# Cosformer attention and token/channel mixer: tokens laid five to a row on 64 partitions and four on the other 64

## The chip, the cores and the metric

The kernel runs on one core of one Trainium2 chip. The metric is the device time of one execution in microseconds (us); lower is better. A profile of one execution stands beside the times. Its span is the time from the first to the last instruction; the execution's own time is a little longer. Engines are named as in the profile: PE (TensorE matmul), PEld (its weight load), DVE (VectorE), ACT (ScalarE), POOL (GpSimd), SP (SyncE, which here issues most DMAs); "POOLq" and "SPq" are their queues of DMA issues.

## The reference, cut to what matters

Eight batches, eight heads, 576 tokens, head dimension 64. Queries and keys become features of width 128, a linear attention follows, and its output goes through a mixer over tokens and one over channels.

```python
cos_w, sin_w = cos(pi/2 * pos / 576), sin(pi/2 * pos / 576)       # per token
phi(x) = concat([relu(x) * cos_w, relu(x) * sin_w])               # 64 -> 128
kv  = einsum('bhsf,bhsd->bhfd', phi(k), v)
z   = sum over s of phi(k)
x   = einsum('bhsf,bhfd->bhsd', phi(q), kv) / (phi(q) . z + 1e-6) # -> [8, 576, 512]
u   = x + (relu(x^T @ w_tok1) @ w_tok2)^T                         # 576 -> 256 -> 576, tokens
out = u + relu(u @ w_ch1) @ w_ch2                                 # 512 -> 1536 -> 512, channels
```

q, k, v and the output are float32 in HBM; the matmuls take bf16.

## The kernel before

**Tokens.** 576 tokens are 4 x 128 + 64. The first 512 (`SM`) lie four to a row (`R = 4`): partition p holds tokens 4p to 4p+3, and "chunk" ci (0 to 3) is the token ci of every row. The last 64 (`ST`) are chunk `R`, the tail. `load_main` (L85) brings a batch's 512 tokens of a tensor in one DMA over 128 rows, with runs of 1024 B for each head and row. `load_tail` (L91) brings its 64 tail tokens in another DMA with runs of 256 B: an even batch into rows 0 to 63 of a tail tile, an odd batch into rows 64 to 127 of the same tile. So a pair of batches shares a tail tile, and from batch 2 on one feature instruction over 128 rows serves the tails of both.

**Front of a batch** (`class Front`). `feature` (L247) computes one half (cos or sin) of the features of one chunk of q or k: on DVE, or on ACT with `on_act`. `values` (L267) casts v into `v_aug`, which has a column of ones; `kv` (L310) accumulates phi(k)^T v on PE; `kv_out` copies it to SBUF. Queries are turned to have features on the partitions: on PE for batches 0 and 1 (`q_trans`, L335), by a DMA transpose on SP for the others (`q_trans_dma`, L351). `num` (L356) multiplies them with kv and divides; `tok1` and `tok2` are the token mixer, `u_trans_dma` and `tail_trans_dma` (L437, L442) turn its result u for the channel mixer.

**Channel mixer** (`class Channel`). A batch has 12 c steps (`c_main`, u^T by w_ch1, 1536 wide in blocks of 128, ReLU on ACT) and then o steps (`o_step`, two matmuls of 512 columns by w_ch2 each). When a chunk is complete, DVE adds u and SP issues the store. The tails of a pair go through the channel mixer together, with the odd batch.

**Order.** The kernel runs under a manual schedule: each engine takes its instructions in the order in which the program emits them. `Front.pieces` (L461) is a list of (slot, piece): the pieces of batch b+1 are emitted behind step `slot` of batch b's channel mixer (slots 0 to 11 are c steps, `C`; from `O = NCH = 12` they are o steps). The tokens' chunks go in `ORDER = (0, 1, 2, R, 3)`. Loads for later batches are emitted in the main loop (L725 to L748) behind given steps; all go to SP's queue. Batch 0's front is `first_front` (L621), the lead-in; four weight loads for w_ch1 are issued on POOL behind k of batch 0 (L188, L192), and three for w_ch2 (L194) behind q of batch 1. `permute_tok2` (L210) casts w_tok2 and orders its columns by chunk, on ACT.

**Batch 1.** Its pieces are in the plan of L471 to L481. `KS`, `QS` are features of k and q, `QT` the turning on PE, `V` values, `KV` the product, `before.tok2` the token mixer's second half of batch 0.

Of the kernel before, what the change touches and what calls it, by code (L numbers as in the profile page):

```python
# [16 lines left out]
def kernel(  # L17
# [67 lines left out]
    def load_main(dst, src, b, lo=0, hi=H, eng=nc.sync):  # L85
        return eng.dma_start(
            out=dst[:, lo:hi, 0:R * D].rearrange("p h (r d) -> p h r d", r=R),
            in_=src[b, lo:hi, 0:SM, :].rearrange("h (p r) d -> p h r d", r=R))


    def load_tail(dst, src, b):  # L91
        return nc.sync.dma_start(out=dst[half(b % 2)],
                                 in_=src[b, :, SM:S, :].rearrange("h s d -> s h d"))

    def tiles():
        return tuple(io.tile([P, H, R * D], F32, name=n) for n in ("qt", "vt", "kt"))

    def tail_tiles():
        return tuple(io.tile([P, H, D], F32, name=n) for n in ("qtt", "vtt", "ktt"))

    io_tiles, io_tails = {0: tiles()}, {0: tail_tiles()}
    qt0, vt0, kt0 = io_tiles[0]
    qtt0, vtt0, ktt0 = io_tails[0]
    load_main(qt0, q, 0, 0, HH)
    load_main(qt0, q, 0, HH, H, nc.scalar)
    load_tail(qtt0, q, 0)
    load_main(kt0, k, 0, 0, HH)
    k_done = load_main(kt0, k, 0, HH, H)
    load_tail(ktt0, k, 0)
    load_main(vt0, v, 0, 0, HH)  # L110
    load_tail(vtt0, v, 0)
    load_main(vt0, v, 0, HH, H)

# [4 lines left out]
    nc.sync.dma_start(out=w_tok1n, in_=moe_w_tok1[0:SM, :].rearrange("(p r) t -> p r t", r=R))  # L118
# [14 lines left out]
    nc.gpsimd.iota(pos_i[:, 0:R], pattern=[[1, R]], base=0, channel_multiplier=R)  # L133
    for g in range(2):
        nc.gpsimd.iota(pos_i[half(g), R:NSC], pattern=[[1, 1]], base=SM, channel_multiplier=1)
# [19 lines left out]
    v_augs, x_tails = [], []  # L155
    for i in range(2):
        va = const.tile([P, NSC, H, DP], BF16, name=f"v_aug{i}")
        nc.vector.memset(va[:, 0:R, :, D:D1], 1.0)
        nc.vector.memset(va[half(1 - i), R, :, :], 0.0)
        nc.vector.memset(va[half(i), R, :, D:D1], 1.0)  # L160
        v_augs.append(va)
        xt = const.tile([P, Dm], BF16, name=f"x_tail{i}")
        nc.vector.memset(xt[half(1 - i), :], 0.0)
        x_tails.append(xt)

    class Tail:

        def __init__(self, pair):
            self.qt, self.vt, self.kt = io_tails[pair]
            self.kp = twos.tile([P, H, 2, D], BF16, name="kp_tail")  # L170
            self.qp = once.tile([P, H, 2, D], BF16, name="qp_tail")
            self.qpT = twos.tile([P, H, P], BF16, name="qpT_tail")
# [7 lines left out]
    for t in (tail0.kp, tail0.qp):  # L180
        nc.gpsimd.memset(t[half(1)], 0.0)
    for g in range(2):
        nc.gpsimd.dma_start(out=w_tail1[half(g), :], in_=moe_w_tok1[SM:S, :])
# [9 lines left out]
    def load_w_ch2(behind):  # L193
        done = [nc.gpsimd.dma_start(  # L194
            out=w_ch2[:, ki:ki + 4, :],
            in_=moe_w_ch2[ki * P:(ki + 4) * P, :].rearrange("(n t) d -> t n d", t=P))
            for ki in range(0, NCH, 4)]
        after(done[0], behind)
        return done
# [10 lines left out]
    def permute_tok2(ki):  # L210
        nc.scalar.copy(w_tok2[:, ki, 0:SM].rearrange("t (r p) -> t r p", r=R),
                       w_tok2n[:, ki, 0:SM].rearrange("t (p r) -> t r p", r=R))
        nc.scalar.copy(w_tok2[:, ki, SM:].rearrange("t (g s) -> t g s", g=2),
                       w_tok2n[:, ki, None, SM:S].to_broadcast([P, 2, ST]))


    class Front:
        def __init__(self, b, res, tail):
# [4 lines left out]


            self.alone = b < 2
            self.kp, self.qp = {}, {}
# [4 lines left out]

        def k_of(self, ci):
            return self.kp[ci] if ci < R else self.tail.kp

        def q_of(self, ci):
            return self.qp[ci] if ci < R else self.tail.qp
# [10 lines left out]
        def feature(self, which, ci, j, heads=(0, H), on_act=False):  # L247
            lo, hi = heads
            w = (cos_t, sin_t)[j][:, ci:ci + 1]
            if ci < R:  # L250
                dst, src = (self.kp, self.kt) if which == "k" else (self.qp, self.qt)
                if ci not in dst:
                    dst[ci] = phi.tile([P, H, 2, D], BF16, name=which + "p")
                o_ap = dst[ci][:, lo:hi, j, :]
                i_ap = src[:, lo:hi, ci * D:(ci + 1) * D]
            else:
                t = self.tail
                dst, src = (t.kp, t.kt) if which == "k" else (t.qp, t.qt)
                rows = self.rows if self.alone else slice(0, P)
                w, o_ap, i_ap = w[rows], dst[rows, lo:hi, j, :], src[rows, lo:hi, :]  # L260
            if on_act:
                nc.scalar.activation(o_ap, i_ap, AF.Relu, bias=bias0[0:w.shape[0]], scale=w)
            else:
                nc.vector.tensor_scalar(o_ap, i_ap, scalar1=w, scalar2=0.0,  # L264
                                        op0=ALU.mult, op1=ALU.max)

        def values(self, ci, eng, heads=(0, H)):  # L267
            lo, hi = heads
            if ci < R:
                src = self.vt[:, lo:hi, ci * D:(ci + 1) * D]  # L270
            else:
                src = self.tail.vt[self.rows, lo:hi, :]
            dst = self.va[self.rows_of(ci), ci, lo:hi, 0:D]
            if eng is nc.scalar:
                nc.scalar.copy(dst, src)  # L275
            else:
                eng.tensor_copy(dst, src)

        def ksum(self, ci, heads=(0, H)):
# [5 lines left out]
            for h in range(*heads):  # L285
                nc.tensor.matmul(self.ks_ps[:, h:h + 1],
                                 self.k_of(ci)[:, h, :, :].rearrange("p a b -> p (a b)"),
# [22 lines left out]
        def kv(self, ci, halves=(0, 1)):  # L310
# [8 lines left out]
            for g in halves:  # L319
                for j in range(HH):  # L320
                    nc.tensor.matmul(self.kv_ps[g][:, j * DP:j * DP + D1],  # L321
                                     self.k_of(ci)[:, g * HH + j, :, :]
# [13 lines left out]
        def q_trans(self, ci, heads=(0, H), eng=nc.scalar):  # L336
            lo, hi = heads
            if hi - lo == H:
                qT_ps = ps_at.tile([P, H, P], BF16, name="qT_ps", tag="at")
            else:  # L340
                qT_ps = ps_mm.tile([P, HH, P], BF16, name="qT_ps", tag="mm")
            for h in range(lo, hi):
                nc.tensor.transpose(qT_ps[:, h - lo, :],
                                    self.q_of(ci)[:, h, :, :].rearrange("p a b -> p (a b)"), ident)
            dst = self.qpT[:, ci * H + lo:ci * H + hi, :] if ci < R else self.tail.qpT[:, lo:hi, :]
# [5 lines left out]
        def q_trans_dma(self, ci):  # L351
            dst = self.qpT[:, ci * H:(ci + 1) * H, :] if ci < R else self.tail.qpT
            nc.sync.dma_start_transpose(out=dst,
                                        in_=self.q_of(ci).rearrange("p h a b -> p (h a b)"))
# [90 lines left out]
        def k_side(self, ci, on_act=False):  # L445
            self.feature("k", ci, 0)
            self.feature("k", ci, 1, on_act=on_act)

        def q_side(self, ci, on_act=False):
            self.feature("q", ci, 0)  # L450
            self.feature("q", ci, 1, on_act=on_act)
# [9 lines left out]
        def pieces(self, b, before):  # L461
# [6 lines left out]
            if first:  # L468

                last = NCH - 1  # L470
                plan = [(4, KS, 0), (5, KS, 1, True), (6, KS, 2, True), (6, KS, 3, True), (7, KS, R),  # L471
                        (8, QS, 0), (9, QS, 1), (9, QT, 0), (10, QS, 2), (10, QT, 1)]
                plan += [(last, *what) for what in (
                    (QS, 3, True), (QT, 2, (0, H), nc.vector), (before.tok2, 2, None, False),
                    (QS, R, True), (QT, 3), (before.tok2, 3, None, False),
                    (QT, R, (0, H), nc.vector), (before.tok2, R, None, False))]
                plan += [(last, V, ci, eng) for ci, eng in enumerate(
                    (nc.gpsimd, nc.gpsimd, nc.scalar, nc.scalar, nc.vector))]
                plan += [(last, KV, ci) for ci in range(NSC)]
                plan.append((last, self.kv_out))  # L480
                plan += [(5, before.tok2, 0, ps_at, False), (7, before.tok2, 1, ps_at, False)]  # L481
            else:
                plan = [(C + at, V, ci, nc.scalar) for ci, at in enumerate((-1, -1, 0, 1, 2))]
                plan += [(C + at, KS, ci) for ci, at in enumerate((0, 0, 1, 2, 2))
                         if ci < R or not odd]
                for ci, at in zip(ORDER, (1, 2, 3, 4, 5)):
                    if ci < R or not odd:
                        plan += [(C + at, QS, ci), (C + at, self.q_trans_dma, ci)]
# [6 lines left out]
            elif odd:  # L495
                at, mix, t = (C + 8, C + 9, C + 11, O + 1, O + 3), O + 4, O + 8
# [20 lines left out]
    class Channel:  # L517
# [39 lines left out]
        def o_step(self, ci, lo, hi, cols=slice(0, Dm)):  # L557
# [12 lines left out]
            if ci < R:  # L570
                nc.sync.dma_start(
                    out=out[b, 0:SM, cols].rearrange("(p r) d -> p r d", r=R)[:, ci, :], in_=o_sb)
                return
            for g in range(2):
                nc.sync.dma_start(out=out[b - 1 + g, SM:S, cols], in_=o_sb[half(g)])
# [206 lines left out]
```

## Time and profile before

Three executions took 276.12, 276.8 and 278.76 us; the median is 276.8.

| | |
|---|---|
| profiled execution | 275.45 us, span 273.6, 5130 instructions |
| granted PE clock | 1.00 throughout |
| HBM read, written | 35.85 MB, 9.44 MB |
| mean DMA rate | 196 GB/s |
| DMA packets | 91816, of them 59409 under 512 B |

Where the time lies by stage: the lead-in runs to about 24 us, where batch 0's c steps begin; its o steps begin at 43.95; from there a batch takes some 30 us (a pair 60.3); the last matmul ends at 270.0.

The page's table of engines gives busy time, its share of the span and the count of instructions. The costliest groups of PE show what it works on:

```profile
L564 PE MATMUL o_ps<-w_ch,h1T 128*128 128x512 bf16 (+1 forms) x396 | 94.8, 372 | 0.0
L531 PE MATMUL c_ps<-uT,w_ch 128*128 128x512 bf16 (+2 forms) x384 | 91.6, 372 | 1.0 <-DMA uT<-u_bf 1.0
```

Such a line has the kernel's line number, the engine and operation, the tiles written and read, shapes and count; then the busy time in us and the mean ns of one; then the engine's idle time ahead of the group and what ended most of it.

The chain of waits follows the work back from the last instruction, at each step to what released it. An answer over windows has, for each stretch of the span, the busy time and number of instructions of each engine, PE's granted clock, the mean share in which the 16 DMA engines were busy (it can be above 1, since packets overlap), and the bytes moved.

### The profile page before, as it was taken

What the parts mean: (1) busy time and instruction counts of PE and PEld (TensorE: products, weight loads), DVE (VectorE), ACT (ScalarE), POOL (GpSimd) and SP (SyncE); (2) the same over time, 40 slices, a digit from 0 to 9 for tenths busy, and PEclk for the clock granted to TensorE, in tenths of its full rate; (3) what the DMA queues carried; (4) which work ended last, traced back from release to release, by engine and by line L of the source; (5) the groups of instructions that cost most, each with busy time, mean ns of one, the idle gap of its engine ahead of it and who ended that gap; (6) DMA issues with size and microseconds to landing.
All of it is one profiled execution on the core that took longest, in us unless ns stands there. A gap on an engine that the chain in (4) does not pass through costs nothing.

```text
span 273.6 us, 5130 instructions
## 1 busy us (share of the span) xinstructions
PE 261.6 (96%) x2050; PEld 138.7 (51%) x2050; DVE 164.7 (60%) x375; ACT 129.8 (47%) x229; POOL 11.2 (4%) x24
## 2 busy tenths in 40 slices
PE   7989987999899999999999999999999999999994
PEld 2665354446554454445654455446644455435543
DVE  6973775774876396659566487659466577720022
ACT  4955982067525184156626183347606372426500
POOL 6400230000000000000000000000000000000000
PEclk9999999999999999999999999999999999999999
DMA  7999999738995897968993969669994361180032
GB/s 222 344 266 283 317 179 283 245 88 264 284 253 185 247 221 191 323 140 233 208 311 79 270 193 259 220 151 237 211 304 119 115 117 38 42 210 0 2 98 94
DMA packets 91816, 53.68 MB, mean 196 GB/s; under 512 B 59409, under 2 KB 86929, under 8 KB 91793
## 3 DMA queue, kind: packets, MB, share of 16 engines
q1 hardware_dynamic: 88432, 49.62, 65.4%
q0 software_dynamic: 2832, 3.21, 7.1%
q10 hardware_dynamic: 528, 0.52, 0.6%
q8 instruction: 16, 0.26, 0.4%
q14 instruction: 8, 0.06, 0.1%
HBM read 35.85 MB, written 9.44 MB: 166 GB/s over the span
## 4 chain that ended last, share of the span: by engine, by line
PE 80%; DMA 7%; DVE 7%; ACT 2%; issue 1%; SPq 0%; DVEq 0%
PE o_ps L564 31%; PE c_ps L531 23%; PE b_ps L385 6%; PE u_ps L409 5%; PE num_ps L362 4%; PE ct_ps L551 4%; DMA qpT<-qp 4%; PE kv_ps L321 3%; DVE qp L264 2%; DMA uT<-u_bf 2%; DMA qt<-in_q_dram 2%; DVE kp L264 2%; PE idle_ps L205 1%; PE c_ps L541 1%; DVE u_sb L412 1%
## 5 line engine op out<-in xcount | busy, mean ns | idle before, releaser
L564 PE MATMUL o_ps<-w_ch,h1T 128*128 128x512 bf16 (+1 forms) x396 | 94.8, 372 | 0.0
L531 PE MATMUL c_ps<-uT,w_ch 128*128 128x512 bf16 (+2 forms) x384 | 91.6, 372 | 1.0 <-DMA uT<-u_bf 1.0
L535 ACT ACTIVATE h1T<-c_ps 128x512 bf16<-128x512 f32 x93 | 55.4, 598 | 57.1 <-PE c_ps L531 56.9
L564 PEld LDWEIGHTS <-h1T 128*128 128x128 bf16 x396 | 37.0, 97 | 38.8
L531 PEld LDWEIGHTS <-w_ch 128*128 128x128 bf16 x384 | 33.3, 97 | 31.2 <-DMA uT<-u_bf 2.0
L569 DVE TENSOR_TENSOR o_sb<-o_ps,u_sb 128x512 f32<-128x512 f32 (+1 forms) x33 | 22.2, 673 | 32.7 <-PE o_ps L564 32.7
L412 DVE TENSOR_TENSOR u_sb<-u_ps,x_sb 128x512 f32<-128x512 f32 x32 | 22.0, 689 | 7.3 <-PE u_ps L409 6.8
L416 ACT CAST u_bf<-u_sb 128x512 bf16<-128x512 f32 x28 | 17.3, 618 | 17.8 <-DVE u_sb L412 16.1
L390 ACT ACTIVATE B<-b_ps 128x512 bf16<-128x512 f32 x8 | 4.8, 597 | 39.5 <-PE b_ps L385 39.5
L409 PE MATMUL u_ps<-B,w_tok 128*128 128x512 bf16 x80 | 22.5, 379 | 0.0
L372 DVE TENSOR_TENSOR x_sb<-num_ps,den 128x512 bf16<-128x512 f32 x28 | 19.4, 691 | 1.0
L551 PEld LDWEIGHTS <-w_ch 128*128 128x128 bf16 x192 | 14.0, 98 | 9.2
L264 DVE TENSOR_SCALAR qp<-qt,cos_t 128x512 bf16<-128x512 f32 (+1 forms) x35 | 15.9, 453 | 4.6 <-DMA qt<-in_q_dram 4.6
L385 PE MATMUL b_ps<-x_sb,w_tok 128*128 128x512 bf16 x64 | 17.9, 379 | 0.0
L264 DVE TENSOR_SCALAR kp<-kt,cos_t 128x512 bf16<-128x512 f32 x32 | 15.2, 480 | 3.9 <-DMA kt<-in_k_dram 3.9
L551 PE MATMUL ct_ps<-uT_tail,w_ch 128*128 128x128 bf16 x192 | 17.2, 219 | 0.0
L275 ACT CAST v_aug<-vt 128x512 bf16<-128x512 f32 (+1 forms) x30 | 16.7, 586 | 0.1
L264 DVE TENSOR_SCALAR qp<-qt,sin_t 128x512 bf16<-128x512 f32 (+1 forms) x34 | 15.7, 460 | 0.0
L362 PEld LDWEIGHTS <-qpT 128*128 128x128 bf16 x256 | 11.5, 98 | 7.1 <-DMA qpT<-qp 1.5
L362 PE MATMUL num_ps<-kv_sb,qpT 128*128 128x65 bf16 x256 | 13.1, 193 | 1.7 <-DMA qpT<-qp 0.7
L569 DVE TENSOR_TENSOR o_sb<-o_ps,u_tail 128x512 f32<-128x512 f32 x4 | 2.8, 692 | 20.0 <-PE o_ps L564 20.0
L321 PE MATMUL kv_ps<-v_aug,kp 128*128 128x65 bf16 x256 | 12.5, 193 | 2.2 <-ACT v_aug L275 1.7
(96 smaller groups left out, 220.9 us busy)
## 6 DMA issues: line engine op xcount, KB each, us to landing
out_dram<-o_sb SPq DMA_DIRECT2D x31, 256.0 KB, 2.9
kt<-in_k_dram SPq DMA_DIRECT2D x7, 1024.0 KB, 6.9
qt<-in_q_dram SPq DMA_DIRECT2D x7, 1024.0 KB, 8.6
vt<-in_v_dram SPq DMA_DIRECT2D x7, 1024.0 KB, 6.5
w_ch<-in_moe_w_ch_dram POOLq DMA_DIRECT2D x4, 384.0 KB, 10.4
w_ch<-in_moe_w_ch_dram POOLq DMA_DIRECT2D x3, 512.0 KB, 8.3
out_dram<-o_sb SPq DMA_DIRECT2D x10, 128.0 KB, 2.3
qtt<-in_q_dram SPq DMA_DIRECT2D x8, 128.0 KB, 5.9
```

The source lines that it names most:

```text
L264: nc.vector.tensor_scalar(o_ap, i_ap, scalar1=w, scalar2=0.0, op0=ALU.mult, op1=ALU.max)
L321: nc.tensor.matmul(self.kv_ps[g][:, j * DP:j * DP + D1], self.k_of(ci)[:, g * HH + j, :, :] .rearrange("p a b -> p (a b)"), self.va[:, ci, ...
L362: nc.tensor.matmul(num_ps[:, g, j * DP:j * DP + D1], self.qT_of(ci, h), self.kv_sb[g][:, j, 0:D1], start=True, stop=True)
L372: nc.vector.tensor_mul(self.x_of(ci)[rows].rearrange("p (g j d) -> p g j d", g=2, j=HH), nv[:, :, :, 0:D], den.to_broadcast([rows.stop - r ...
L385: nc.tensor.matmul(self.b1_ps[mi], w, self.x_of(ci), start=(ci == ORDER[0]), stop=(ci == ORDER[-1]))
L409: nc.tensor.matmul(u_ps, w_tok2[:, ki, ci * P:(ci + 1) * P], self.B1[:, ki, :], start=(ki == 0), stop=(ki == NT - 1))
L412: nc.vector.tensor_add(u, u_ps[rows], self.x_of(ci)[rows])
L531: nc.tensor.matmul(c_ps[:, lo:hi], w_ch1[:, ki, mi * P:(mi + 1) * P], uT[:, lo // P:hi // P, ki, :], start=(ki == 0), stop=(ki == NCC - 1))
L535: nc.scalar.activation(self.h1T[:, mi, :], c_ps, AF.Relu)
L551: nc.tensor.matmul(self.ct_ps[:, mi % R, :], w_ch1[:, ki, mi * P:(mi + 1) * P], self.tail.uT[:, ki, :], start=(mi % R == 0 and ki == 0), s ...
L564: nc.tensor.matmul(o_ps, h, w_ch2[:, ki, cols], start=ki == 0, stop=ki == NCH - 1)
L569: nc.vector.tensor_add(o_sb, o_ps, u)
```

## The change

- **Layout.** Rows 0 to 63 hold five tokens each (tokens 0 to 319), rows 64 to 127 four each (320 to 575). Chunk 4 (`R`) is now the fifth token of rows 0 to 63, in every batch. Each load of q, k or v is two DMAs of 64 rows, with runs of 1280 B and 1024 B; there are no tail tiles and no tail loads. w_tok1's load and every 128-row store are two DMAs of 64 rows as well. The tables of positions, the tail of w_tok1 and the order of w_tok2's columns follow (`permute_tok2` has three ACT instructions per block instead of two).
- **Tail work.** Each batch computes the features of its own chunk R on 64 rows, and each odd batch too has its own transpose of them. The tiles `kp_tail` and `qpT_tail` become two constant tiles each, whose unused parts are zeroed once on DVE in the setup (four memsets, among them two of 128 rows); the two memsets on POOL at L181 go.
- **Batch 1's pieces.** The sin features of k's chunks 0 to 3 and of q's chunks 2 and 3 go to POOL, that of q's chunk 1 to ACT; values 0 to 3 all go to POOL. The k features come one or two slots earlier. The three issues of w_ch2's load on POOL are emitted in slot 6, behind the k features. The pieces of `before.tok2` move, and its chunk R comes behind `kv_out`.
- **Odd batches.** The third, fourth and fifth num pieces, the token mixer and the turning of u come one slot earlier.
- **Third batch's query.** Its load (batch 2) is emitted one o step later, at `NCH + 17`, behind one more store.

```diff
-    def load_main(dst, src, b, lo=0, hi=H, eng=nc.sync):
-        return eng.dma_start(
-            out=dst[:, lo:hi, 0:R * D].rearrange("p h (r d) -> p h r d", r=R),
-            in_=src[b, lo:hi, 0:SM, :].rearrange("h (p r) d -> p h r d", r=R))
-    def load_tail(dst, src, b):
-        return nc.sync.dma_start(out=dst[half(b % 2)],
-                                 in_=src[b, :, SM:S, :].rearrange("h s d -> s h d"))
+    SL = ST * NSC
+    HALVES = ((half(0), slice(0, SL), NSC), (half(1), slice(SL, S), R))
+    def load(dst, src, b, lo=0, hi=H, eng=nc.sync):
+        return [eng.dma_start(out=dst[rows, lo:hi, 0:r * D],
+                              in_=src[b, lo:hi, toks, :].rearrange("h (p r) d -> p h (r d)", r=r))
+                for rows, toks, r in HALVES]
+    def by_rows(ap, rows, toks, r):
+        return ap[toks, :].rearrange("(p r) d -> p r d", r=r)
...
-    nc.sync.dma_start(out=w_tok1n, in_=moe_w_tok1[0:SM, :].rearrange("(p r) t -> p r t", r=R))
+    for half_of in HALVES:
+        nc.sync.dma_start(out=w_tok1n[half_of[0]], in_=by_rows(moe_w_tok1, *half_of)[:, 0:R, :])
...
+        kp = const.tile([P, H, 2, D], BF16, name=f"kp_tail{i}")
+        nc.vector.memset(kp[half(1)], 0.0)
+        kp_tails.append(kp)
+        qpT = const.tile([P, H, P], BF16, name=f"qpT_tail{i}")
+        nc.vector.memset(qpT, 0.0)
+        qpT_tails.append(qpT)
...
-    for t in (tail0.kp, tail0.qp):
-        nc.gpsimd.memset(t[half(1)], 0.0)
...
-        nc.scalar.copy(w_tok2[:, ki, 0:SM].rearrange("t (r p) -> t r p", r=R),
-                       w_tok2n[:, ki, 0:SM].rearrange("t (p r) -> t r p", r=R))
-        nc.scalar.copy(w_tok2[:, ki, SM:].rearrange("t (g s) -> t g s", g=2),
-                       w_tok2n[:, ki, None, SM:S].to_broadcast([P, 2, ST]))
+        main = w_tok2[:, ki, 0:SM].rearrange("t (r p) -> t r p", r=R)
+        for rows, toks, r in HALVES:
+            nat = w_tok2n[:, ki, toks].rearrange("t (p r) -> t r p", r=r)
+            nc.scalar.copy(main[:, :, rows], nat[:, 0:R, :])
+            if r > R:
+                nc.scalar.copy(w_tok2[:, ki, SM:].rearrange("t (g s) -> t g s", g=2),
+                               nat[:, R:r, :].to_broadcast([P, 2, ST]))
...
-                plan = [(4, KS, 0), (5, KS, 1, True), (6, KS, 2, True), (6, KS, 3, True), (7, KS, R),
-                        (8, QS, 0), (9, QS, 1), (9, QT, 0), (10, QS, 2), (10, QT, 1)]
-                plan += [(last, *what) for what in (
-                    (QS, 3, True), (QT, 2, (0, H), nc.vector), (before.tok2, 2, None, False),
-                    (QS, R, True), (QT, 3), (before.tok2, 3, None, False),
-                    (QT, R, (0, H), nc.vector), (before.tok2, R, None, False))]
-                plan += [(last, V, ci, eng) for ci, eng in enumerate(
-                    (nc.gpsimd, nc.gpsimd, nc.scalar, nc.scalar, nc.vector))]
-                plan += [(last, KV, ci) for ci in range(NSC)]
-                plan.append((last, self.kv_out))
-                plan += [(5, before.tok2, 0, ps_at, False), (7, before.tok2, 1, ps_at, False)]
+                dve, act, pool = nc.vector, nc.scalar, nc.gpsimd
+                T0, every = before.tok2, (0, H)
+                plan = [(3, KS, 0, pool), (4, KS, 1, pool), (5, T0, 0, ps_at, False),
+                        (5, KS, 2, pool), (6, KS, 3, pool), (6, KS, R), (6, load_w_ch2),
+                        (7, T0, 1, ps_at, False), (8, QS, 0), (8, QS, 1, act),
+                        (9, QT, 0), (9, QS, 2, pool), (10, QT, 1, every, dve), (10, QS, 3, pool),
+                        (11, QT, 2), (11, QS, R), (11, T0, 2, None, False),
+                        (11, QT, 3, every, dve), (11, T0, 3, None, False), (11, QT, R, every, dve)]
+                plan += [(11, V, ci, pool) for ci in range(R)]
+                plan.append((11, V, R, dve))
+                plan += [(11, KV, ci) for ci in range(NSC)]
+                plan += [(11, self.kv_out), (11, T0, R, None, False)]
...
-                at, mix, t = (C + 8, C + 9, C + 11, O + 1, O + 3), O + 4, O + 8
+                at, mix, t = (C + 8, C + 9, C + 10, C + 11, O + 2), O + 3, O + 7
...
-            if ci < R:
-                nc.sync.dma_start(
-                    out=out[b, 0:SM, cols].rearrange("(p r) d -> p r d", r=R)[:, ci, :], in_=o_sb)
-                return
-            for g in range(2):
-                nc.sync.dma_start(out=out[b - 1 + g, SM:S, cols], in_=o_sb[half(g)])
+            for g, half_of in enumerate(HALVES):
+                of = (out[b], *half_of) if ci < R else (out[b - 1 + g], *HALVES[0])
+                nc.sync.dma_start(out=by_rows(*of)[:, ci, cols], in_=o_sb[half(g)])
...
-            if b == 0 and i == NCH + 16:
+            if b == 0 and i == NCH + 17:
                 load_batch(2, "q")
```

## The prediction

> **What bounds the kernel now.** I read the page's busy shares and chain first, then the span in stretches, then single rows where TensorE (PE) idles. The page:
>
> ```profile
> PE 261.6 (96%) x2050; PEld 138.7 (51%) x2050; DVE 164.7 (60%) x375; ACT 129.8 (47%) x229; POOL 11.2 (4%) x24
> PE 80%; DMA 7%; DVE 7%; ACT 2%; issue 1%; SPq 0%; DVEq 0%
> ```
>
> PE is the bound: 12 of 273.6 us are idle, and 3.6 of those are the last add and stores. The stretches (window, length, busy time of PE, PEld, DVE, ACT, POOL with counts, granted clock, DMA share, GB/s) say where the rest is:
>
> ```profile
> 5.00:20.00 15.00, 13.35 (x226) 9.09 (x224) 12.33 (x36) 11.57 (x23) 3.21 (x4) 1.00 1.13 312
> 30.00:43.90 13.90, 10.79 (x111) 6.17 (x110) 10.16 (x20) 11.43 (x18) 3.88 (x5) 1.00 1.11 220
> 60.00:74.00 14.00, 12.44 (x134) 7.89 (x134) 9.04 (x22) 8.31 (x16) 0.00 (x0) 1.00 0.97 264
> 95.00:155.40 60.40, 60.27 (x453) 31.28 (x452) 39.73 (x89) 28.64 (x51) 0.00 (x0) 1.00 0.82 216
> ```
>
> 1.65 us in the lead-in, 3.11 in the stage of batch 1's pieces, 1.56 where batch 2 waits for q, almost nothing over a pair of batches. In the first two the DMA share is above 1.1: there, bytes and their rate are the limit. The rows that end the waits (start, us, engine, what, idle before and its end):
>
> ```profile
> 18.92 1.13 ACT L211 CAST w_tok<-u_sb 128x512 bf16<-128x512 f32 x1 [2.07 <-DMA u_sb<-in_moe_w_tok_dram]
> 28.58 0.49 DVE L264 TENSOR_SCALAR kp<-kt,cos_t 128x512 bf16<-128x512 f32 x1 [3.58 <-DMA kt<-in_k_dram]
> 36.11 1.40 POOL L277 CAST v_aug<-vt 128x512 bf16<-128x512 f32 x2 [1.04 <-DMA vt<-in_v_dram]
> 67.30 0.49 DVE L264 TENSOR_SCALAR qp<-qt,cos_t 128x512 bf16<-128x512 f32 x1 [4.08 <-DMA qt<-in_q_dram]
> ```
>
> All four wait for a load, so the price of a load is the first question.
>
> **The split loads.** The same bytes come in fewer pieces, but each transfer writes 64 rows. The nearest rows:
>
> ```profile
> 5.40:5.80 0.40, 0.06 (x1) 0.00 (x0) 0.40 (x2) 0.40 (x1) 0.00 (x0) 1.00 1.35 289
> 24.50:25.90 1.40, 1.40 (x8) 0.66 (x7) 0.49 (x1) 0.00 (x0) 0.00 (x0) 1.00 1.09 382
> 261.50:262.70 1.20, 1.20 (x8) 0.51 (x6) 0.47 (x1) 0.00 (x0) 0.00 (x0) 1.00 0.90 210
> 266.20:267.00 0.80, 0.80 (x6) 0.32 (x5) 0.00 (x0) 0.00 (x0) 0.00 (x0) 1.00 0.78 305
> ```
>
> In order: a 64-row tail load, 289 GB/s; the 128-row load of k, 382; two 64-row stores, 210 at share 0.90, so 233 at a full share; a 128-row store, 305 at 0.78, so 391. Before, a tensor costs 1.049 MB at 382 plus 0.131 MB at 289: 2.75 + 0.45 = 3.20 us. After, 1.180 MB costs 3.09 us at 382, 4.08 at 289, 5.06 at 233: -0.1, +0.88 or +1.86 a tensor. I take 289, the one row that is a load to 64 rows; 382 and 233 stay as ends. (The tail's packets are 256 B, which may slow it; the stores move the other way. Each flaw points to one end.)
>
> The Trainium skill, "SBUF — State Buffer", section "Door 1: The DMA port swizzle", says that rows 0–63 reach half of the ports, 196 GB/s against 328 for 128 rows, and under "Can I just issue two DMAs to hit both halves?" that two halves serialize. By the page's figures alone a tensor would cost an estimated 6.0 us. The stores agree (233 against 391); the tail load at 289 does not, though for 0.4 us only.
>
> *Lead-in.* DVE gains four memsets of 512 words. The row of 320 words takes 0.33, so 0.53 each and 0.06 between: +2.36. The two POOL memsets at L181 (0.95, 0.97) go, and the DVE line beside them ends with the first one:
>
> ```profile
> 1.90 0.99 DVE L142 TENSOR_SCALAR theta<-theta 128x5 f32<-128x5 f32 x1
> 1.92 0.95 POOL L181 MEMSET kp_tail<- 64x1024 bf16 x1
> 5.40 0.35 DVE L264 TENSOR_SCALAR qp<-qt,cos_t 128x256 bf16<-128x256 f32 x1 [0.52 <-DMA qt<-in_q_dram]
> ```
>
> If it takes 0.17, as the DVE cast ahead of it, -0.82. Setup ended at 4.88, so DVE is free at 6.42 and the first feature starts 1.0 later. Batch 0's k lands 2 x 0.88 later (12.1 against 10.3) and that covers the memsets, which alone would cost 0.7 (1.0 less 0.36 that DVE waits for k today). w_tok2 comes behind three tensors and the split w_tok1 (0.524 MB, +0.44): 18.92 + 2.64 + 0.44 = 22.0. The permutations run 18.92 to 21.46, just in time for the B activation; in two more pieces some 0.4 longer, so B and the c steps behind it come at +3.1 + 0.4 = 3.5.
>
> *Batch 1's pieces.* The chain has c blocks from 24.26; the o steps begin at 43.95: 19.7 us, 3.1 idle, so 16.6 of PE work. With the c blocks at 27.8 that work alone would end at 44.4. The other limit is v: ready at 36.1 today, behind six tensors and w_tok1, so 36.1 + 5.3 + 0.4 = 41.8; then four casts on POOL at 0.70 (the row above, 1.40 for two) and the last KV chunk, about 0.3: 44.9. The later governs: +0.95. Below this are hidden the k sin features on POOL (the page has no such row; between 0.70, the cast, and 1.4, twice it; I take 0.9, and 3.6 for four lies in the PE work ahead of the queries, which land 1.8 or more behind k), the ACT feature of q (0.70 in the chain), and w_ch2's three issues (2.48 on POOL). These issues now stand behind four features, and the o steps need only their first third at first: landed near 40 today, with 3 to 4 to spare.
>
> *Third batch's query.* The load's issue passes one o step (0.86 at 0.43 a matmul) and two store issues (0.5 each at most, only one of them new work), less the two tail issues that went (1.31 for both, one half behind q itself). I count +0.9 to issue and +0.88 to land, against 0.95 by which everything else is late already: relative to PE, +0.9. That stage idles with the last transposes, so it is paid in full. Uncertain by 0.7 both ways.
>
> *Odd batches.* Four more DVE features (0.40 apart, 1.6 us) and one more DMA transpose (1.26 on SP) in batches 3, 5, 7; DVE is busy 39.7 of 60.4 us there and PE idles 0.13, so 0; if DVE's kv_sb copy becomes last, 0.25 a batch. PE transposes on 64 rows save nothing that waits. The uT transposes now follow each other; in the last batch a store issue lay between them and PE waited 0.61: -0.6. Stores as two issues: +0.45 each in DMA time (0.262 MB at 233 against 391), hidden until the end, where the last store goes out in one more issue (0.34 to 0.57): +0.45. uT of batch 1 goes out behind later loads: +0.4, between 0 and 1.5.
>
> *Steady state.* Six tensors at +0.88 and eight stores at +0.45 raise the DMA share of a pair from 0.82 by 8.9/60.4 to 0.97. Stretches at 0.97 (60 to 74) do work, with waits for loads alone: 0.
>
> Sum: 0.95 + 0.9 + 0.4 - 0.6 + 0.45 = +2.1 us. From the profiled 275.45, that is 277.6; the median is 1.35 above the profiled run, so **278.9**. The other uncertain sizes give +1 to +4: 277.8 to 280.8.
>
> **Rivals.** *Half-row loads at the stores' rate (slower).* +1.86 a tensor: v ready at 36.1 + 11.2 + 0.9 = 48.2 if no other transfer fills in, o steps at 51; with overlap 48, so +4 to +7. The third batch's q adds 1.9 more than PE's delay. The pair's share becomes 0.82 + (11.2 + 3.6)/60.4 = 1.06, close to the 1.11 and 1.13 at which PE idled: 0 to 2 a pair. In all +5 to +14, typically +7: 284. It decides from about 260 GB/s down. For it: both store windows. Against: 289 on the load itself.
>
> *The loads cost no more (no slower).* At 382 the c blocks come 0.7 later, v 0.6 earlier, and the stage's 3.1 idle can close: PE's work ends at 24.96 + 16.6 = 41.6, -2.4, or nothing where POOL's features or casts are last. With q of batch 2 -0.5 to +0.9, the ends -0.15, and the lead-in's 1.65 idle, which may lose 1 with the tail loads out of its queue: -4 to +0.75, or 272.8 to 277.6. For it: the 1024 B packets cost 46 ns in the records, which no longer 256 B pieces interrupt; against: the DVE memsets are certain.
>
> *POOL against DVE.* The theta row holds DVE for as long as POOL's memset runs; DVE features of k and q beside POOL's features could do the same. Eight features at 1.4 with DVE blocked half the time: 8 x 0.7 = 5.6, of which the idle 3.1 hides part: +2.5 over the free case, 280 with unharmed loads, 281.5 with mine. The Trainium skill, "SBUF — State Buffer", section "Who interferes with whom", calls it an exclusive lock. Today's DVE features beside POOL's casts (0.47) do not show it; beside POOL's descriptor work 0.61.
>
> *The change does what it says:* the tail loads and their issues are gone from the program, so I give nothing to that rival.
>
> **How the numbers follow.** Forecast 0.40, store-rate loads 0.26, unharmed loads 0.26, POOL lock 0.08. 1%, 2.8 us, is about what a measurement of this kernel can tell from no change: 274.0 to 279.6. The forecast splits 0.29 same, 0.11 slower; store-rate loads are all slower; unharmed loads 0.12 faster, 0.14 same; the lock 0.03 same, 0.05 slower. Faster 0.12, same 0.46, slower 0.42. The range 273.2 to 285.5 leaves out the upper 0.10 of the store-rate case and 0.05 of the unharmed one at its end.
>
> **What would show it.** Wait rows of DVE for k and q and of ACT for w_tok2 give the load price: w_tok2 at 22 (289), 24 or more (233), 19 (382). DMA GB/s in a stretch where only a load runs. First feature at 6.4. O steps of batch 0 at 44.9. POOL features in a row of their own, DVE features beside them at 0.48 or longer. Idle PE between 95 and 215 us would show a saturated queue. I am wrong if the load's rate lies at either end, or if a wait shows up in the pairs.

## The result and the profile after

The changed kernel takes 294.95 us (median of 4, 294.3 to 296.92) where the kernel before takes 276.56 (median of 4 beside it): 1.066 times the time, with a 95% interval of 1.0583 to 1.0737. The forecast of 278.9 and its range up to 285.5 were too low; slower had been given 0.42. The profiled execution took 294.57, span 292.8. Ratios and intervals here are of fast executions alone, while a median can include a slow one (it does for load_halves, load_evenodd and both_evenodd), so small differences are read from the ratios.

The same stretches as before, from the answer over windows (window, length, busy time of PE, PEld, DVE, ACT, POOL with counts, granted clock, DMA share, GB/s):

```profile
5.00:20.00 15.00, 11.26 (x142) 7.22 (x143) 10.50 (x32) 8.66 (x18) 3.08 (x4) 0.89 1.11 237
40.00:50.00 10.00, 4.46 (x24) 2.33 (x24) 5.71 (x11) 3.50 (x5) 9.97 (x7) 0.83 0.81 143
80.00:84.00 4.00, 0.70 (x7) 0.31 (x4) 1.28 (x4) 1.11 (x3) 0.00 (x0) 1.00 1.11 218
84.00:88.00 4.00, 3.55 (x27) 2.22 (x28) 4.00 (x11) 0.92 (x2) 0.00 (x0) 0.57 1.12 240
100.00:160.00 60.00, 58.48 (x442) 30.55 (x445) 40.55 (x92) 27.81 (x50) 0.00 (x0) 1.00 1.01 212
```

Three things are to be seen. The lead-in moves 237 GB/s where it moved 312, at the same DMA share of 1.11 to 1.13: the DMA engines are as busy and carry less. From 40 to 50 us POOL is busy for 9.97 of 10 us and PE for 4.46. From 80 to 84 PE stands almost still, and in the next 4 us its clock is at 0.57; before, the clock was 1.00 throughout. PE's own wait there names a feature of k on DVE:

```profile
PE kv_ps L303 <- DVE kp L249: 3.8, 1, 3.8
```

That feature stands behind the first two features of batch 2's query on DVE, and those wait for the query's load (the last row of the next table).

The rows that end the waits, at the same places as before:

```profile
25.00 0.66 ACT L210 CAST w_tok<-u_sb 128x256 bf16<-128x256 f32 x1 [2.37 <-DMA u_sb<-in_moe_w_tok_dram]
36.48 1.32 DVE L249 TENSOR_SCALAR kp<-kt,cos_t 128x512 bf16<-128x512 f32 x2 [5.34 <-DMA kt<-in_k_dram]
36.74 8.81 POOL L249 TENSOR_SCALAR kp<-kt,sin_t 128x512 bf16<-128x512 f32 x4 [19.42 <-DMA kt<-in_k_dram]
45.50 2.42 POOL L192 DMA_DIRECT2D w_ch<-in_moe_w_ch_dram  x3
47.94 4.05 POOL L249 TENSOR_SCALAR qp<-qt,sin_t 128x512 bf16<-128x512 f32 x2
51.95 2.28 POOL L259 CAST v_aug<-vt 128x512 bf16<-128x512 f32 x4
82.72 0.48 DVE L249 TENSOR_SCALAR qp<-qt,cos_t 128x512 bf16<-128x512 f32 x1 [7.57 <-DMA qt<-in_q_dram]
```

w_tok2 lands at 25.0 (18.9 before), batch 1's k at 36.5 (28.6). From there POOL works without a gap until 54.2: four features in 8.81, so 2.2 us each, then w_ch2's issues, two more features in 4.05, four casts. The chain of waits (start, us, what) goes through them:

```profile
12.87 12.12 DMA u_sb<-in_moe_w_tok_dram
...
30.41 2.59 PE c_ps L526 x12
...
38.83 6.72 POOL kp L249 x3
...
47.94 4.06 POOL qp L249 x2
...
56.00 0.86 PE o_ps L549 x4
```

The c blocks begin at 30.41 (24.26 before), the o steps at 55.84 by the timeline (43.95): 6.2 and 11.9 us later. So of the 19.2 us between the two spans, 11.9 are lost by the first o step and 3.5 where batch 2's query is awaited (it is 26.9 us behind the first o step, 23.35 before). Of the rest, the low clock from 84 to 88 is worth an estimated 1.5 (0.43 of the 3.55 us in which PE was busy), one later wait for a turned query takes 1.3, and the end 0.9.

### The profile page after: what moved, and what is told of

The parts are those of the page before. It is cut to its first block, busy times and chain, and to the rows that moved or that the text cites. A ratio compares the mean times of both kernels' runs of the same rounds, so it can differ in the third digit from the quotient of the medians.

```text
span 292.8 us, 5195 instructions
## 1 busy us (share of the span) xinstructions
PE 267.1 (91%) x2029; PEld 141.9 (48%) x2050; DVE 171.9 (59%) x390; ACT 124.6 (43%) x224; POOL 22.8 (8%) x29
## 4 chain that ended last, share of the span: by engine, by line
PE 67%; DMA 16%; DVE 5%; POOL 4%; issue 2%; SPq 2%; ACT 2%; POOLq 0%; DVEq 0%
PE o_ps L549 27%; PE c_ps L516 19%; PE u_ps L395 6%; PE b_ps L371 5%; DMA qpT<-qp 4%; DMA u_sb<-in_moe_w_tok_dram 4%; DMA kt<-in_k_dram 3%; PE ct_ps L536 3%; DMA qt<-in_q_dram 3%; DMA uT<-u_bf 2%; PE num_ps L348 2%; PE kv_ps L303 2%; POOL kp L249 2%; DVE x_sb L358 2%; POOL qp L249 1%
## 5 line engine op out<-in xcount | busy, mean ns | idle before, releaser
L516 PE MATMUL c_ps<-uT,w_ch 128*128 128x512 bf16 (+2 forms) x384 | 94.2, 379 | 1.5 <-DMA uT<-u_bf 1.5
L549 PE MATMUL o_ps<-w_ch,h1T 128*128 128x512 bf16 (+1 forms) x382 | 93.1, 372 | 0.6
L249 DVE TENSOR_SCALAR qp<-qt,cos_t 128x512 bf16<-128x512 f32 (+2 forms) x43 | 19.8, 464 | 10.5 <-DMA qt<-in_q_dram 10.5
L249 DVE TENSOR_SCALAR kp<-kt,cos_t 128x512 bf16<-128x512 f32 x32 | 16.2, 515 | 5.8 <-DMA kt<-in_k_dram 5.8
L257 ACT CAST v_aug<-vt 128x512 bf16<-128x512 f32 (+2 forms) x34 | 19.3, 591 | 0.1
L249 DVE TENSOR_SCALAR qp<-qt,sin_t 128x512 bf16<-128x512 f32 (+2 forms) x40 | 18.4, 460 | 0.0
L326 PE MATMUL qT_ps<-ident,qp 128*128 128x128 bf16 (+1 forms) x80 | 8.5, 257 | 9.4 <-DVE qp L249 6.2
```

The lines of the kernel that those rows point to most:

```text
L249: eng.tensor_scalar(o_ap, i_ap, scalar1=w, scalar2=0.0, op0=ALU.mult, op1=ALU.max)
L516: nc.tensor.matmul(c_ps[:, lo:hi], w_ch1[:, ki, mi * P:(mi + 1) * P], uT[:, lo // P:hi // P, ki, :], start=(ki == 0), stop=(ki == NCC - 1))
L549: nc.tensor.matmul(o_ps, h, w_ch2[:, ki, cols], start=ki == 0, stop=ki == NCH - 1)
```

## The experiments

Two theories had the price of a load in common and differed in its cause: *rows* (64 neighbouring rows load at about 235 GB/s, whatever else) or *cutting* (two transfers for one, odd packet sizes, more issues). A third question was what the GpSimd features cost by themselves, and what depended on late loads. Each comparison ran beside the kernel before, at 276.8 to 277.1 us.

### Prices alone (rates)

A kernel with the loads of two tensors in six forms, one form behind the other, then stores in three forms, then features; one execution.

> Measures prices alone; computes nothing of the reference. Two 1 MiB loads in each of six forms, one form behind the other: 128 rows; lower and upper 64 rows as two transfers; even and odd rows as two transfers; five tokens on the lower rows and four on the upper; four transfers of 32 rows; lower rows from SP's queue and upper rows from ACT's at once. If it is the 64 neighbouring rows that make a load slow, the second, fourth and fifth form show about 235 GB/s (the 237 of the changed kernel's lead-in) and even and odd rows about 380, as 128 rows do. If it is the cutting into two transfers, even and odd rows are at 235 too. If 1280 B packets are to blame, only the fourth form is slow. Then GpSimd features of 128x512 alone and beside VectorE's: if the lock between the two engines made them 2.2 us in the changed kernel, alone they take 0.7 to 1.2; if the operation itself is dear there, about 2 us alone too.

Windows inside five of the load forms (here DVE, ACT and POOL busy, then PE's clock, DMA share, GB/s): 128 rows; halves; even and odd rows, twice; five and four tokens; lower rows from SP's and upper rows from ACT's queue:

```profile
6.00:10.50 4.50, 1.45 (x9) 0.00 (x0) 0.00 (x0) 1.00 1.10 363
14.00:22.00 8.00, 1.23 (x8) 0.00 (x0) 0.00 (x0) 1.00 1.12 221
23.00:24.60 1.60, 1.19 (x8) 0.00 (x0) 0.00 (x0) 1.00 1.10 349
27.20:28.80 1.60, 0.00 (x1) 0.00 (x0) 0.00 (x0) 1.00 1.07 348
35.00:38.00 3.00, 1.09 (x8) 0.00 (x0) 0.00 (x0) 1.00 1.11 221
55.00:59.00 4.00, 1.23 (x8) 1.28 (x1) 0.00 (x0) 1.00 1.10 222
```

Halves 221 GB/s, 128 rows 363, even and odd rows 349 with as many transfers as the halves. The five-and-four form is no worse than halves with 1024 B runs, so packet size is not it; two queues don't help. Four transfers of 32 rows gave 216. The halves also read other addresses of HBM than the even and odd rows do, which no run separates; but the 128-row form reads neighbouring addresses too, at 363, so neighbouring addresses alone are not slow.

The Trainium skill, "SBUF — State Buffer", section "Door 1: The DMA port swizzle", gives a contiguous 0–63 as reaching half of the ports and 196 GB/s at 1 MiB; the direction agrees with 221 against 363. Its section "Can I just issue two DMAs to hit both halves?" says that only one transfer over all 128 partitions reaches all ports; the 64 even rows at 349 GB/s do not bear that out, while its port formula, which looks at bits of the row number, would allow them.

POOL's rows of the same kernel (start, us; four features alone, four beside DVE's, three casts, three multiplications, three maxima):

```profile
64.23 8.28 POOL L114 TENSOR_SCALAR y<-x,w 128x512 bf16<-128x512 f32 x4 [63.80 <-DVE z L109]
77.09 9.58 POOL L114 TENSOR_SCALAR y<-x,w 128x512 bf16<-128x512 f32 x4 [3.96 <-DVE y L125]
87.18 1.97 POOL L134 CAST y<-x 128x512 bf16<-128x512 f32 x3
89.24 4.88 POOL L136 TENSOR_SCALAR y<-x,w 128x512 bf16<-128x512 f32 x3
94.22 4.63 POOL L138 TENSOR_SCALAR y<-x 128x512 bf16<-128x512 f32 x3
```

A feature takes 2.07 us on POOL alone and 2.4 beside DVE's; a cast 0.66, one operation 1.5 to 1.6. DVE did the same feature in 0.52 alone (8 in 4.13) and 0.57 beside POOL (16 in 9.18). The operation itself is dear on POOL; DVE's work beside it adds 0.3.

### GpSimd features back on VectorE and ACT (feat_back)

```diff
-                plan = [(3, KS, 0, pool), (4, KS, 1, pool), (5, T0, 0, ps_at, False),
-                        (5, KS, 2, pool), (6, KS, 3, pool), (6, KS, R), (6, load_w_ch2),
+                plan = [(3, KS, 0, dve), (4, KS, 1, act), (5, T0, 0, ps_at, False),
+                        (5, KS, 2, act), (6, KS, 3, act), (6, KS, R), (6, load_w_ch2),
...
-                        (9, QT, 0), (9, QS, 2, pool), (10, QT, 1, every, dve), (10, QS, 3, pool),
+                        (9, QT, 0), (9, QS, 2, dve), (10, QT, 1, every, dve), (10, QS, 3, act),
```

> The changed kernel with batch 1's six GpSimd features back on VectorE and ACT. If the loads alone carry the loss, the o steps of batch 0 still begin near 55 (v lands where it did) and the time stays at 292 to 296. If the GpSimd features carry half of it, the o steps begin at 48 to 50 and the time falls to 286 to 290. If they carry nearly all, 280 or less.

290.28 us, 1.0476 (1.0435 to 1.0516): 4.7 less than the changed kernel. The o steps begin at 52.0, 3.85 earlier. That lies between two of the answers: just above the 286 to 290 that stood for half of the loss, and with later o steps than its 48 to 50. The features carry a quarter of the loss; the rest stays with them gone.

### The kernel before with its loads in halves, and in even and odd rows (load_halves, load_evenodd)

```diff
     def load_main(dst, src, b, lo=0, hi=H, eng=nc.sync):
-        return eng.dma_start(
-            out=dst[:, lo:hi, 0:R * D].rearrange("p h (r d) -> p h r d", r=R),
-            in_=src[b, lo:hi, 0:SM, :].rearrange("h (p r) d -> p h r d", r=R))
+        return [eng.dma_start(
+            out=dst[half(g), lo:hi, 0:R * D],
+            in_=src[b, lo:hi, g * R * ST:(g + 1) * R * ST, :].rearrange("h (p r) d -> p h (r d)", r=R))
+            for g in range(2)]
...
```

and in the other kernel

```diff
+            out=dst[g:P:2, lo:hi, 0:R * D],
+            in_=src[b, lo:hi, 0:SM, :].rearrange("h (p two r) d -> two p h (r d)", two=2, r=R)[g])
...
```

> The kernel before with each 128-row load of q, k and v cut into two transfers, rows 0 to 63 and 64 to 127, and nothing else. If 64 neighbouring rows load at 235 GB/s, the loads' stretch of the lead-in falls from about 380 to 240 GB/s, v of batch 1 lands 8 to 11 us later and the time is 283 to 290. If the split as such costs only issues, 277 to 279.

> The same cut into two transfers, but even rows and odd rows. If the neighbouring rows are the cause, this is 276 to 279, and the loads run at about 380 GB/s; if two transfers in place of one are the cause, it is as slow as the cut into halves.

Halves: 286.97 us, 1.0329 (1.0263 to 1.0395). Even and odd rows: 278.61 us, 1.0044 (1.0014 to 1.0075). The same bytes, packets (to within one of 92249), transfers and issues; only the rows differ, with the tokens that lie on them. The lead-in and the first o step of the one and then of the other:

```profile
5.00:20.00 15.00, 12.83 (x156) 7.90 (x155) 9.12 (x29) 9.40 (x18) 3.14 (x4) 0.89 1.14 246
50.52 1.37 PE L565 MATMUL o_ps<-w_ch,h1T 128*128 128x512 bf16 x4
```

```profile
5.00:20.00 15.00, 12.80 (x202) 8.45 (x201) 10.22 (x33) 11.86 (x24) 7.26 (x4) 1.00 1.08 297
45.45 1.03 PE L565 MATMUL o_ps<-w_ch,h1T 128*128 128x512 bf16 x4
```

246 against 297 GB/s; the o steps begin at 50.5 and 45.45. Rows are the cause, and cutting alone costs some 0.4%.

### Stores in halves, and both (store_halves, both_halves, both_evenodd)

```diff
-                nc.sync.dma_start(
-                    out=out[b, 0:SM, cols].rearrange("(p r) d -> p r d", r=R)[:, ci, :], in_=o_sb)
+                for g in range(2):
+                    nc.sync.dma_start(
+                        out=out[b, 0:SM, cols].rearrange("(p r) d -> p r d", r=R)[half(g), ci, :],
+                        in_=o_sb[half(g)])
```

both_halves has this and the loads in halves; both_evenodd has loads and stores over `[g:P:2]`.

> The kernel before with each 128-row store cut into rows 0 to 63 and 64 to 127. If the stores' slower rate (233 for 391 GB/s) is hidden but for the last one, the time is 277 to 277.5. If it delays loads and transposes in the queue, 278 to 280.

> The kernel before with loads and stores cut into halves. If the halves of both add up, load_halves' 287.0 plus what store_halves costs. If they compete for the same queue, more than the sum; with 290 or more, nearly all that the changed kernel loses without its GpSimd features (290.3) is the halves, and the other edits are worth about nothing.

> The kernel before with each 128-row load and each 128-row store cut into two transfers of even and odd rows: as many transfers and issues as both_halves (292.1), on other rows. If only the rows matter, 278 to 280 (load_evenodd's 278.6 and the stores' issues); if the number of transfers matters as much, 285 or more.

store_halves 279.86 (1.0095, 1.0065 to 1.0125): not hidden. PE waits 2.2 us for transposes of u, 1.0 before. both_halves 292.1 (1.0538, 1.0485 to 1.0592): more than the sum of 3.3% and 0.95%, though the ends of the intervals meet, and as slow as feat_back within the intervals. both_evenodd 281.17 (1.017, 1.0096 to 1.0244), between the two answers: over load_evenodd the stores cost some 3 us there as well, so what a cut store costs seems to be its second issue on SP, not its rows. In rates, stores over even and odd rows kept the DMA engines busy for a share of 0.58 only (213 GB/s), stores in halves for 0.93 (204 GB/s). With both_evenodd's interval that is likely rather than shown.

### The new plan on the old layout (new_plan)

The plan of batch 1 and the place of `load_w_ch2` are copied from the changed kernel; layout, loads and stores are those of before.

> The kernel before, its layout and loads kept, with the changed kernel's plan for batch 1: six features and four values on GpSimd, w_ch2's issues behind the four k features. A GpSimd feature takes 2.07 us alone. If what it costs depends on the loads being late, the o steps of batch 0 begin no more than 1 us later than 43.95, and the time is 276 to 278. If the GpSimd chain sets the end by itself, then k at 28.6, four features, w_ch2's issues, two features and four casts (28.6 + 8.8 + 2.4 + 4.1 + 2.6) end at 46.5, and the o steps begin at 46.5 to 47: 279 to 280.

280.64 us, 1.0124 (1.008 to 1.0169). POOL's timeline:

```profile
28.54 8.64 POOL L264 TENSOR_SCALAR kp<-kt,sin_t 128x512 bf16<-128x512 f32 x4 [15.05 <-DMA kt<-in_k_dram]
37.14 2.29 POOL L196 DMA_DIRECT2D w_ch<-in_moe_w_ch_dram  x3
39.45 4.17 POOL L264 TENSOR_SCALAR qp<-qt,sin_t 128x512 bf16<-128x512 f32 x2
43.57 2.28 POOL L277 CAST v_aug<-vt 128x512 bf16<-128x512 f32 x4
```

k is there at 28.5, as before, and POOL still ends at 45.9. The o steps begin at 47.95, 4.0 later. The GpSimd chain sets the end of this stage by itself, without any late load.

### The later load of batch 2's query (feat_back_q16)

feat_back with `NCH + 16` in place of `NCH + 17`.

> feat_back with the load of batch 2's query emitted one o step earlier again, as in the kernel before. If the later issue (18.7 us behind the first o step in the changed kernel, 17.35 before) is paid where PE waits for that query, 1 to 1.5 us less than feat_back's 290.3; if the half-row transfers alone set its landing, 290 again.

289.08 us, 1.0433 (1.0393 to 1.0472), 1.2 under feat_back, as the first answer has it; but the intervals overlap, and of the two profiled executions the one with the earlier load took longer (290.26 against 289.67), so the gain is not settled.

### Two parts that gain (odd_early, values_pool, odd_and_values)

```diff
-                at, mix, t = (C + 8, C + 9, C + 11, O + 1, O + 3), O + 4, O + 8
+                at, mix, t = (C + 8, C + 9, C + 10, C + 11, O + 2), O + 3, O + 7
```

```diff
-                    (nc.gpsimd, nc.gpsimd, nc.scalar, nc.scalar, nc.vector))]
+                    (nc.gpsimd, nc.gpsimd, nc.gpsimd, nc.gpsimd, nc.vector))]
```

The first is odd_early, the second values_pool, both on the kernel before; odd_and_values has both.

> The kernel before with the odd batches' num pieces, token mixer and turning one slot earlier, as in the changed kernel, and nothing else. If the store between two transposes in the last batch is what PE waits for (0.61 us), 276.2; if it changes nothing else, between 276.0 and 277.

> The kernel before with the four casts of batch 1's values all on GpSimd (two were on ACT), taken from the changed kernel's plan. Before, PE waits 1.65 us for ACT's cast ahead of kv; on GpSimd the four end at 36.1 + 4 x 0.70 = 38.9, ahead of the turning of the queries. If that wait is what ends the stage, it goes: 275 to 276. If ACT's casts only hid another wait (the query's last transposes), 276.5 to 277.

> odd_early and values_pool together. If the two gains are apart in time and add: 274.5 to 275.5; if the first is noise, as values_pool.

276.39 (0.997, 0.9945 to 0.9995), 275.62 (0.9936, 0.9911 to 0.9961) and 274.72 us (0.9913, 0.988 to 0.9946). In the last, kv's matmuls run through, but for 0.46 us, and the o steps begin at 42.73 instead of 43.95 (PE's timeline):

```profile
40.88 1.15 PE L321 MATMUL kv_ps<-v_aug,kp 128*128 128x65 bf16 x32
42.49 0.40 PE L321 MATMUL kv_ps<-v_aug,kp_tail 128*128 128x65 bf16 x8 [0.46 <-DVE v_aug L277]
42.73 1.03 PE L564 MATMUL o_ps<-w_ch,h1T 128*128 128x512 bf16 x4
```

This is faster than both kernels, made of two small parts of the change on the layout of before.

## Why the prediction was wrong

**The load price, the step that decided.** "I take 289, the one row that is a load to 64 rows." The loads ran at 221 alone and 237 in the lead-in; the stores' 233, kept as the other end, was the right row. The two rows were also read differently: the stores' 210 was divided by its DMA share of 0.90, the tail load's 289 was not divided by its 1.35, which gives 214. That row covers 0.4 us and 0.12 MB, and its 256 B packets had been noted as a flaw that would make it too *slow* a guide. A row of 0.4 us was put above a row of 1.2 us. By 221, a tensor costs 1.18 / 0.221 = 5.3 us, +2.1 instead of +0.88. The path from there was right in the main: the rival at the stores' rate said o steps at 48 to 51 and a time of about 284; load_halves has 50.5 and 286.97. The sign named for it, w_tok2 at 24 or later, came too: 25.0.

**The GpSimd features, the second miss.** The prediction: "the page has no such row; between 0.70, the cast, and 1.4, twice it; I take 0.9", hidden in other work. They take 2.07 alone (rates), above the upper bound; a cast is no bound for an operation with two arithmetic steps, and one step alone takes 1.5. POOL then becomes the chain that ends last: +3.85 us at the o steps, 4.7 in time (feat_back), and +4.0 and some 3.5 even with the old loads (new_plan). The rival with POOL gave a feature 1.4 and the loss to a lock between the engines; beside DVE's features DVE went from 0.52 to 0.57 only.

**w_ch2's issues.** "3 to 4 to spare" was enough: no o step waits for w_ch2. What stands behind does move: k and v of batch 2 go out behind w_ch2's second third, at 54.3 instead of 41.7 (51.9 in feat_back). The trace shows no wait that follows from it: DVE's first k feature of that batch begins at 72.70 with no idle time ahead of it.

**The DVE memsets** were sized right: 6.42 forecast, 6.44 measured (the last begins at 5.96 and takes 0.48), and theta takes 0.17 with POOL's memset gone. They cost nothing, as DVE then waited 2.58 us more for q (first feature 9.03, forecast 6.4).

**Third batch's query.** Forecast +0.9 relative to PE, measured +3.5: the issue comes 18.7 behind the first o step instead of 17.35 (+1.4), and the landing another 2.1 later (8.1 us from issue to the first feature, 6.0 before). The issue was forecast at +0.9 and the landing at +0.88, the wrong load price. The 0.95 that the forecast took off again is a slip: the load is issued behind o steps and moves with PE, so its own two terms say +1.8.

**Odd batches and the end.** The earlier turning in odd batches: -0.6 forecast, -0.7 measured on the layout of before (odd_early, interval -1.5 to -0.1). In the changed kernel the gain is not to be seen: PE's waits for turned u sum to 1.5 us there, 1.0 before. The last stores: +0.45 forecast; from the end of the last add to the end of the span 4.04 us, 3.15 before, so +0.9.

**Stores** were counted as "hidden until the end". They cost 2.8 us on the layout of before (store_halves). In its profile 1.2 us of that are waits for transposes, which stand behind the stores on SP, and 1.0 is the end (4.14 us behind the last add, 3.15 before); the rest is not placed.

**Steady state.** The DMA share rose to 1.01 (forecast 0.97), and PE lost 1.5 us from 100 to 160, 1.3 of it in one wait for a turned query, and 0.6 in the next 60, where 0 had been forecast. A small miss, and the sign that the prediction had named: a wait in the pairs.

**PE's clock** was not in the sum at all. It is low behind stretches in which PE stands still for long: 0.66 from 9 to 14 us (PE busy 1.20 of the 4 us ahead of it), 0.83 from 40 to 50, 0.57 from 84 to 88. PE's busy time rose from 261.6 to 267.6 us in load_halves, with the same matmuls, and only to 262.6 in load_evenodd; the changed kernel's 267.1 lacks some 20 records. The Trainium skill, "TensorE: Matmul & The Clock Gate", part 1, says that an idle window of about 3.4 us halves the clock; here PE stood still for 3.8 us, and 0.57 followed, which agrees. How much of the 18.4 us between the medians this is was not tried by itself, but executions of one program allow an estimate: load_halves took 285.05 us at a mean granted clock of 1.000 and 288.2 at 0.982, so 1.75 us for a hundredth. At that price the 0.976 of the changed kernel's profiled execution is worth some 4 us. They are a part of what the waits cost, not another loss beside them.

**Do the parts add?** By the ratios, loads in halves cost 3.3%, stores 0.95%, POOL's features 1.8%, the later query about 0.4%: 6.5%, against 6.6% measured. But both_halves alone is 5.4% and not 4.2%, so the parts seem to interact, and the other edits (no tail loads, the earlier turning) would then give something back. Their sum is settled no closer than some 2 us. A layout with five tokens on rows that spread over both halves was not tried: chunk R would have to be computed on rows that are not neighbours.

## What to carry to other kernels

Before a 128-row transfer is cut, ask which rows each piece writes: 64 neighbouring rows ran at 0.61 of the rate of 128 (221 to 363 GB/s), 64 alternate rows at 0.96 (349). When two rows of a profile price an unknown, read both by the same measure and prefer the one that lasted over the one of the same name. For an operation that the profile does not hold, work the sum out with a bound well above the nearest row as well. An engine at 4% busy is not free capacity until one instruction of the kind has been timed on it.

## What the hardware showed that was not expected

64 even rows load at 349 GB/s in a transfer of the same size and count as the lower 64 rows at 221. GpSimd's two-step feature on 128x512 takes 2.07 us where its cast takes 0.66; the Trainium skill, "GPSIMD Engine Reference", introduction, has VectorE roughly twice as fast for elementwise work, and here the same feature took VectorE 0.52, a factor of 4. Beside each other the two engines slowed one another by about a tenth and a sixth: 0.57 for 0.52 and 2.4 for 2.07.
